# Attention and a Toeplitz convolution on one core: two further Toeplitz tile buffers, second buffers for the conv's result and taps, a longer planned slack, and a tail in halves

## The chip, the core and the metric

The kernel runs on one core of a Trainium2 chip. The metric is the device time of one execution in microseconds; several executions are timed, and the median is given. A profile is taken of one execution by the hardware profiler. The engines are PE (matmuls; PEld is its weight load), ACT, DVE, POOL, and SP, which here only issues DMAs.

## The reference

Two branches over 2048 tokens with 448 channels are mixed by a gate of each token (bf16 inputs and output):

```
g = sigmoid((x * gate_w).sum(-1, keepdims=True))
a = A(x)      # 16 heads of 28, one shared key and value head: softmax(q k^T / sqrt(28)) v, then @ wo
b = B(x)      # per channel d: K[d,l] = Re sum_n C[d,n] exp(dt*A[d,n]*l) dt*B[d,n], causal conv of x with K, plus x * Dskip
out = g * a + (1 - g) * b
```

In B, n runs over 256 complex modes, and the convolution has the full length of 2048.

## The kernel before, in words

**Attention.** Index i = 0 to 15 stands for a chunk of 512 queries (i // 4) and a group of four heads (i % 4). Its 64 tiles (16 key blocks x 4 heads) give 1024 score tiles in all, taken in sets of three and two in turn. For each set PE computes scores (L1138) into PSUM banks 0 to 5, ACT takes the exponential of the whole set into a ring of 15 slots (L1162, 410 instructions), and PE multiplies by the values with a column of ones for the denominators (L1171) into bank psB. After 16 key blocks `norm(i)` (L1045) copies psB to `acc` (L1051, on ACT) and, for i < 15, sends the denominators through DRAM to come back broadcast: DMA to denT, reciprocal (L1058), DMA to R, DMA to rdenB, multiply to onT (L1062). The DMAs are POOL's. `outp` (L1027) multiplies four onT by Wo, and `fold` (L1039) adds gate times the result to O on DVE (L1042).

**Convolution.** Channels are taken 32 at a time, c = 0 to 13. `masters` and `tables` build powers of the modes on DVE (L848 to L927), `kgen` (L930) sums them to taps on PE (L948), DVE and ACT evict these to `kstg` (L958, L961), and POOL writes them to KP in DRAM. From there `tload` (L974) reads Toeplitz tiles: tile gi = 0 to 111 holds four channels, 128 partitions by 4288 bf16 values, with shifted overlapping reads of KP; SP issues these loads into T, which has NTR = 5 slots, gi % 5. `conv` (L982) takes four tiles: 4 x 8 groups of four matmuls (L995) into one of two PSUM banks that kgen, the query projection `qproj` (L798), outp and conv share; DVE multiplies by 1 - g into `cst` (L1005), PE transposes cst (L1016), and DVE adds to O (L1024). There is one cst, so the first matmul of conv(c) waits for the transposes of conv(c - 1). Channel block 13 is built in two halves (`HALVES`); its tables run in 64 columns at a time.

**Tail.** For i = 15 there is no DMA in norm: DVE copies psB (L1052), PE sums the denominators with selecting columns (L1070), DVE takes reciprocals (L1074) and spreads them to 512 columns (L1076), PE transposes them back (L1081), DVE multiplies (L1085). `tail` (L1088) multiplies the last chunk's onT by Wo for four token tiles: three heads groups early, the fourth after L1085 (both L1103); four folds follow (L1042), then the output DMAs. All four depend on the key ("O", 3), and so on all four folds.

**What sets the order.** Nothing is ordered by hand. `Prog.op` and `Prog.dma` record operations with a cost in ns, keys read and written, and a priority; `schedule` (L147) plays them through and takes again and again the operation that can start first (ties by priority). So each engine's instruction order comes from these costs. An operation of PE with priority 1.2 or more, or DVE with 2 or more, is taken to be ready later than its inputs by a slack, 700 ns on PE and 300 on DVE, unless `slk` names another:

```
if x.pr >= (1.2 if x.eng == "pe" else 2) or x.slk:
    t += self.SLACK.get(x.eng, 0.0) if x.slk is None else x.slk
```

A DMA's cost (L139, L226) is a time on the shared engines plus 2200 ns plus its `extra`; for a T load that is 2584 + 2200 + 2500. `emit` then writes the orders out with semaphore waits. Each engine executes its list in order, so an instruction that waits holds all behind it. `fill` (L616) puts matmuls that add zero (L632) into gaps of PE's plan, to keep its clock up.

Of the kernel before, what the change touches and what calls it, by code (L numbers as in the profile page):

```python
# [11 lines left out]
P = 128  # L12
# [20 lines left out]
NTR = 5  # L33
RING = 15
# [3 lines left out]
NCST = 1  # L38
# [313 lines left out]
def on(i):  # L352
    return i % NON


class Kernel:
# [34 lines left out]
    def alloc(self):  # L391
# [25 lines left out]
        self.T = sb("T", NTR * TW, BF)  # L417
        self.tab = sb("tab", 2 * LO + 32 * EW, BF)
        self.tmp = sb("tmp", 2 * 8 * EW, BF)
# [11 lines left out]
        self.cst = sb("cst", NCST * 512, BF)  # L431
        self.skt = sb("skt", D // 4, BF)
        self.small = sb("small", 16, F32)
        self.gt = sb("gt", 2 * 16, F32)
# [5 lines left out]
    def consts(self):  # L440
# [6 lines left out]
        dm(V(self.kstg, 0, 256), 0.0, 170, [("kst", 0), ("kst", 1)])  # L447
# [33 lines left out]
    def loads(self):  # L481
# [41 lines left out]
        for k in range(2, 6):  # L523
# [7 lines left out]
               (448, 128), "pad", rd=[("kst", 0), ("kst", 1)], wr=["pad"], pr=3)  # L531
# [15 lines left out]
    def prep_x(self):  # L547
# [3 lines left out]
        for q in range(4):  # L551
            for hp in range(2):
# [11 lines left out]
                dst = xT.v(0, DT, 2 * hp * S + 512 * q, [[S, 2], [4, 128], [1, 4]])  # L564
# [9 lines left out]
            def mk(e, q=q, t=t, o=o):  # L574
                for T in range(NT):
                    r = e.matmul(t.v(0, P, o, [[1, 512]]), self.Wk.v(0, DT, T * P, [[1, P]]),
                                 xT.v(0, DT, T * S + 512 * q, [[1, 512]]),
                                 start=(T == 0), stop=(T == 3), tile_position=(0, 0))
                return r
# [9 lines left out]
            def mv(e, q=q):  # L589
                for kt in range(4 * q, 4 * q + 4):  # L590
                    for T in range(NT):
                        r = e.matmul(self.psB.v(0, P, 32 * kt, [[1, 29]]), xT.v(0, DT, T * S + 128 * kt, [[1, 128]]),
# [18 lines left out]
        pg.op("dve", lambda e: e.tensor_scalar(og, g, -1.0, 1.0, ALU.mult, ALU.add), 80, rd=["gt"], wr=["og"], pr=1)  # L611

# [185 lines left out]
    def qproj(self, i):  # L798
# [8 lines left out]
        for T in range(NT):  # L807
            pg.op("pe", lambda e, T=T: e.matmul(
                px(), self.Wq.v(0, DT, T * 512 + g * 128, [[1, 128]]),
                self.xT.v(0, DT, T * S + 512 * qc, [[1, 512]]), start=(T == 0), stop=(T == 3),  # L810
# [119 lines left out]
    def kgen(self, c, sub=None):  # L930
# [9 lines left out]
        k1, k2 = ([(k, h) for h in ((0, 1) if whole else (sub,))] for k in ("kst", "kst2"))  # L940
        for jj in range(8):
# [13 lines left out]
            for comp in range(2):  # L955
                pg.op("pe", lambda e, mm=mm, comp=comp: mm(e, comp), 226 if whole else 113, mode="c", st=2.08 if whole else 1.04,
                      rd=keys, wr=[X] + k1 + k2, pr=1.7, lock=G if jj == 0 and comp == 0 else None)
        pg.op("dve", lambda e: e.tensor_tensor(self.kstg.v(p0, np, 63, [[64, 8]]), G.v(p0, np, 63, [[64, 8]]),  # L958
                                               self.skt.v(p0, np, 8 * c, [[1, 8]]), ALU.add),
              el(8), rd=[X, "skt"], wr=k1, pr=2)  # L960
        pg.op("act", lambda e: e.activation(self.kstg.v(p0, np, 0, [[64, 8], [1, 63]]), G.v(p0, np, 0, [[64, 8], [1, 63]]), AF.Copy),  # L961
              490, rd=[X] + k1, wr=k2, pr=-1, unlock=G)
        ko = self.kstg
        rs = ko.rs
        lst = [(dram(self.KP, (32 * c + 8 * gs[0]) * KW + 1024, [[8 * KW, len(gs)], [KW, 8], [1, 64]]),
                bass.AP(tensor=ko.h, offset=(p0 + 16) * rs, ap=[[32 * rs, len(gs)], [64, 8], [1, 64]]))]
        for g in gs:
            for h in range(2):
                lst.append((dram(self.KP, h * KH + (32 * c + 8 * g) * KW, [[64, 16], [KW, 8], [1, 64]]),
                            ko.v(32 * g + 16 * h, 16, 0, [[64, 8], [1, 64]])))  # L970
        pg.dma(lst, (264 * len(gs), 128), f"kw{sub or 0}", rd=k1 + k2, wr=[("KP", 2 * c + h) for h in ((0, 1) if whole else (sub,))],
               pr=0, eng="pool", extra=2000)

    def tload(self, gi):  # L974
        pg = self.pg
        s = gi % NTR
        x = ["tpdone", "rawdone"] if gi < NTR else []
        pg.dma([(self.T.v(0, P, s * TW, [[1, TW]]),
                 dram(self.KP, 4 * gi * KW, [[1, 64], [KH, 2], [1, TW]]))],
               (128, 2 * TW), f"T{s}", rd=[("KP", gi // 4), "pad"] + x, wr=[("T", s)], pr=1, extra=2500)  # L980

    def conv(self, c):  # L982
        pg = self.pg
        X = ("cx", c)
        co, ck = 512 * (c % NCST), ("cst", c % NCST)
# [3 lines left out]
        for k in range(4):  # L989
            gi = 4 * c + k  # L990
            s = gi % NTR
            for n in range(8):
                def mm(e, k=k, n=n, s=s, gi=gi):
                    for j in range(4):
                        r = e.matmul(ps.v(32 * j, 32 - 2 * n, 128 * k, [[1, 128]]),  # L995
                                     self.U.v(0, P, 2 * n * D + 4 * gi + j, [[D, 32 - 2 * n]]),
                                     self.T.v(0, P, s * TW + j * KW + 896 - 128 * n, [[1, 128]]),
# [5 lines left out]
                      wr=[X] + ([ck] if first else []), pr=1.8,  # L1003
                      lock=ps if first else None)
        pg.op("dve", lambda e: e.tensor_tensor(self.cst.v(0, P, co, [[128, 4], [64, 2], [1, 64]]),  # L1005
# [5 lines left out]
        def yt(e, k):  # L1011
            for par in range(2):
                for mu in (0, 1):
# [3 lines left out]
                                 self.cst.v(0, P, co + 128 * k + 64 * (1 - mu), [[1, 64]]),  # L1017
# [27 lines left out]
    def norm(self, i):  # L1045
# [5 lines left out]
        (pg.op("act", lambda e: e.activation(av, self.psB.v(0, P, 0, [[1, 512]]), AF.Copy), 490, rd=[("b", 6)], wr=[ak], pr=-1) if i < 15 else  # L1051
         pg.op("dve", lambda e: e.tensor_copy(av, self.psB.v(0, P, 0, [[1, 512]])), el(512), rd=[("b", 6)], wr=[ak], pr=0))  # L1052
# [204 lines left out]
```

## Time and profile before

| | |
|---|---|
| runs | 542.43, 543.3, 543.5, 547.04, 548.25 us; median 543.5 |
| profiled execution | 542.43 us, span 540.7 us |
| mean granted PE clock | 0.961 |
| first and last exponential (L1162) | 26.03 us to 528.08 us |
| T loads | 112 of 1072 KB, issued from 94.4 to 511.6 us; issue to landing 5.8 / 10.5 / 20.0 us (least, median, most) |
| conv matmuls (L995) | 2048 into psX, 1536 into psS, 0.24 us each |
| last transposes of the conv (L1016) | end at 527.8 us |

The profile is read so. Busy time of an engine is summed over its instructions; the span is that of the profiled execution. A line like "L1162 ACT ACTIVATE expT<-psS" names a line of the code, the engine, the operation and the tiles it writes and reads; "x410" counts instructions, then come busy us and mean ns of one, then the idle time just before them and who ended most of it. "issue" means that the engine waited for nothing that the profile shows. The granted clock is a share of PE's full clock, the DMA share the mean busy share of the core's 16 DMA engines.

### The profile page before, as it was taken

Reading aid. Unit: us, or ns where it says so; the run is one execution under the profiler, and the core shown is the slowest. Engines: PE = TensorE matmul, PEld = TensorE weight load, DVE = VectorE, ACT = ScalarE, POOL = GpSimd, SP = SyncE. Lnnn points to the kernel's source line nnn. Section 1 sums busy time; section 2 is a strip of 40 time slices with the busy share of each in tenths; the row PEclk is TensorE's granted clock in tenths of the full one; section 3 lists DMA queues with packets and bytes.
Section 4 is the critical chain, followed back from the end, with each engine's and each line's share of the span. In section 5 each row is a group of like instructions: output and inputs, shape, how many; then the busy total and the mean of one; then the engine's idle time right before and its main releaser. Section 6 shows DMA issues by size and latency. Waiting matters only on the chain.

```text
span 540.7 us, 20290 instructions
## 1 busy us (share of the span) xinstructions
PE 485.0 (90%) x9244; PEld 247.4 (46%) x9259; DVE 449.8 (83%) x885; ACT 497.3 (92%) x457; POOL 102.1 (19%) x192
## 2 busy tenths in 40 slices
PE   7689898989999899999899999899988999997984
PEld 4432243344445444554455554454544455553442
DVE  8979999989989799999999999999999997211113
ACT  3799999988989799999999999999999999799890
POOL 2000004003022304004040404022041330401000
PEclk9999999997979799999999989999999999899898
DMA  8931100996945978897877979979978879599954
GB/s 233 283 121 52 31 23 13 342 308 220 365 160 193 347 281 309 325 359 279 337 282 264 313 282 347 359 295 344 359 270 336 280 243 396 159 369 351 392 209 136
DMA packets 38382, 142.88 MB, mean 264 GB/s; under 512 B 10580, under 2 KB 21372, under 8 KB 23960
## 3 DMA queue, kind: packets, MB, share of 16 engines
q1 hardware_dynamic: 27656, 135.29, 69.1%
q0 software_dynamic: 9104, 6.13, 4.5%
q8 instruction: 72, 1.18, 0.9%
q10 hardware_dynamic: 1536, 0.17, 0.3%
q14 instruction: 14, 0.11, 0.1%
HBM read 135.38 MB, written 5.74 MB: 261 GB/s over the span
## 4 chain that ended last, share of the span: by engine, by line
ACT 43%; PE 25%; DVE 17%; DMA 13%; issue 1%; ACTq 0%; another core or an unknown queue 0%
ACT expT L1162 41%; PE psS L1138 7%; DMA T<-KP_scratch 7%; PE psS L948 6%; PE psB L1171 4%; DMA rdenB<-R_scratch 3%; DVE tab L903 2%; PE psS L995 2%; DMA sz<-in_A_wv_dram 2%; PE psX L995 1%; PE psX L948 1%; DVE tab L910 1%; DVE tab L909 1%; DVE tab L922 1%; DVE tmp L905 1%
## 5 line engine op out<-in xcount | busy, mean ns | idle before, releaser
L1162 ACT ACTIVATE expT<-psS 128x1536 bf16<-128x1536 f32 (+1 forms) x410 | 470.8, 1330 | 15.1 <-PE psS L1138 13.9
L1138 PE MATMUL psS<-qT,kT 32*128 32x512 bf16 x1024 | 164.6, 396 | 26.6 <-ACT expT L1162 19.6
L1171 PE MATMUL psB<-expT,vaug 128*32 128x512 bf16 x1024 | 105.2, 401 | 0.7 <-ACT expT L1162 0.3
L1138 PEld LDWEIGHTS psS<-qT,kT 32*128 32x128 bf16 x1024 | 39.4, 91 | 116.3 <-ACT expT L1162 91.6
L137 POOL DMA_DIRECT2D KP_scratch<-kstg x127 | 68.3, 546 | 87.8 <-ACT kstg L961 86.0
L1144 PE MATMUL psB<-ident,zero 32*128 32x512 bf16 x190 | 75.3, 396 | 0.0
L903 DVE TENSOR_TENSOR tab<-tab,mbf 128x256 bf16<-128x256 bf16 (+5 forms) x75 | 69.4, 926 | 1.1
L995 PE MATMUL psX<-T,U 128*26 128x128 bf16 (+7 forms) x2048 | 59.1, 244 | 4.7 <-DMA T<-KP_scratch 3.7
L995 PEld LDWEIGHTS psX<-T,U 128*26 128x26 bf16 (+7 forms) x2048 | 51.1, 162 | 16.9 <-issue 9.0
L632 PE MATMUL psB<-ident,zero 128*32 128x512 bf16 (+3 forms) x808 | 55.6, 337 | 0.2 <-issue 0.2
L1171 PEld LDWEIGHTS psB<-expT,vaug 128*32 128x32 bf16 x1024 | 26.3, 93 | 60.4 <-issue 58.6
L948 PE MATMUL psS<-tab 128*32 128x64 bf16 x1024 | 46.0, 294 | 3.2 <-issue 2.9
L995 PE MATMUL psS<-T,U 128*32 128x128 bf16 (+7 forms) x1536 | 43.4, 241 | 4.2 <-issue 2.7
L995 PEld LDWEIGHTS psS<-T,U 128*32 128x32 bf16 (+7 forms) x1536 | 38.2, 162 | 12.5 <-issue 8.3
L948 PEld LDWEIGHTS psS<-tab 128*32 128x32 bf16 x1024 | 34.2, 138 | 13.7 <-issue 10.4
L905 DVE TENSOR_TENSOR tmp<-tab,mbf 128x256 bf16<-128x256 bf16 (+4 forms) x62 | 39.6, 638 | 0.0
L137 POOL DMA_DIRECT2D denT<-acc x15 | 10.7, 714 | 138.8 <-ACT acc L1051 138.8
L922 DVE TENSOR_TENSOR tab<-tab,tmp 128x2048 bf16<-128x2048 bf16 x28 | 33.5, 1222 | 0.4
L137 POOL DMA_DIRECT2D R_scratch<-denT x15 | 8.7, 578 | 130.0 <-DVE denT L1058 87.9
L948 PE MATMUL psX<-tab 128*32 128x64 bf16 x768 | 31.3, 292 | 0.9 <-issue 0.7
L1005 DVE TENSOR_TENSOR cst<-psX,omq 128x512 bf16<-128x512 f32 x16 | 11.0, 686 | 23.8 <-PE psX L995 23.7
L905 DVE TENSOR_TENSOR tab<-tab,mbf 128x4096 bf16<-128x4096 bf16 x13 | 29.7, 2284 | 0.0
(145 smaller groups left out, 547.6 us busy)
## 6 DMA issues: line engine op xcount, KB each, us to landing
T<-KP_scratch SPq DMA_DIRECT2D x112, 1072.0 KB, 10.6
rdenB<-R_scratch POOLq DMA_DIRECT2D x15, 256.0 KB, 11.9
U<-in_A_x_dram SPq DMA_DIRECT2D x3, 896.0 KB, 15.8
tab<-in_A_x_dram SPq DMA_DIRECT2D x4, 448.0 KB, 7.2
KP_scratch<-kstg POOLq DMA_DIRECT2D x112, 16.0 KB, 5.1
SZ_scratch<-tab SPq DMA_DIRECT2D x1, 1344.0 KB, 5.8
out_dram<-O SPq DMA_DIRECT2D x3, 448.0 KB, 3.8
sz<-SZ_scratch SPq DMA_DIRECT2D x3, 384.0 KB, 3.3
```

Of the source, the lines that this page charges most:

```text
L137: return [e.dma_start(o, i, **kw) for o, i in pairs]
L632: r = e.matmul(t.v(32 * j, 32, bo, [[1, 128 * m]]), self.zero.v(0, P, 0, [[1, 32]]), self.ident.v(0, P, 0, [[0, m], [1, P]]), start=not ac ...
L903: vo(lambda e, dst=dst, src=src, mr=mr: e.tensor_tensor(dst, src, mr, ALU.mult), 2 * n, done + mk(lv), kr + ki)
L905: vo(lambda e, src=src, mi=mi, w=w, n=n, tb=tb, to=to: e.tensor_tensor(tb.v(0, P, to, [[n, 2], [cw, w], [1, cw]]), src, mi, ALU.mult), 2 * ...
L922: vo(lambda e, h=h: e.tensor_tensor(tab.v(0, P, FM + 32 * h, [[64, 2], [EW, 32], [1, 32]]), tab.v(0, P, lo + 31 * EW + 64 * h, [[BLK, 2], ...
L948: r = e.matmul(G.v(32 * g, 32, 64 * jj, [[1, 64]]), tab.v(0, P, lo + comp * BLK + 32 + o, [[EW, 32]]), tab.v(0, P, fo, [[mo - fo, 2], [EW, ...
L995: r = e.matmul(ps.v(32 * j, 32 - 2 * n, 128 * k, [[1, 128]]), self.U.v(0, P, 2 * n * D + 4 * gi + j, [[D, 32 - 2 * n]]), self.T.v(0, P, s ...
L1005: pg.op("dve", lambda e: e.tensor_tensor(self.cst.v(0, P, co, [[128, 4], [64, 2], [1, 64]]), ps.v(0, P, 63, [[128, 4], [64, 2], [-1, 64]]) ...
L1138: r = e.matmul(self.psS.v(0, P, 512 * (bo + k), [[1, 512]]), kT.v(32 * h, 32, 128 * kt, [[1, 128]]), qT.v(32 * h, 32, 512 * (i % 2), [[1, ...
L1144: r = e.matmul(self.psB.v(0, P, 0, [[1, 512]]), self.zero.v(32 * h, 32, 0, [[1, P]]), self.ident.v(32 * h, 32, 0, [[0, 4], [1, P]]), start ...
L1162: pg.op("act", lambda e: e.activation(expT.v(0, P, 512 * es, [[1, n]]), self.psS.v(0, P, 512 * bo, [[1, n]]), AF.Exp, scale=SQ), 50 + n / ...
L1171: r = e.matmul(self.psB.v(32 * h, 32, 0, [[1, 512]]), vaug.v(0, P, 32 * kt, [[1, 32]]), expT.v(0, P, 512 * (t % RING), [[1, 512]]), start= ...
```

## The change

- **Toeplitz slots.** `self.tslots` holds the five slots of T, a sixth in xT (columns 1856 to 6143, from tile 70 on) and a seventh at the start of tab (from tile 96 on). `slot` gives a tile the slot used longest ago among those open to it. The first load into either new slot waits for the last readers of the old contents: the query projections of the first three quarters of xT, and the readers of the even tables. To this end xT is laid out by quarters of tokens (2048 q + 512 T in place of 2048 T + 512 q), and all its readers are changed to match.
- **Second buffers.** Odd c in `conv` uses xT columns 0 to 511 as cst, odd c in `kgen` uses columns 512 to 1023 as kstg. Both wait, at c = 1, for the readers of xT's first quarter.
- **Slack.** The first group (n = 0) of matmuls on each Toeplitz tile gets slk = 2500.
- **Gate into the normalisation for i = 12 to 15.** Two small DMAs on SP write the last chunk's gates to DRAM and read them back as gtT; for i = 12 to 14 denT is multiplied by it. The tail then needs no gate.
- **norm(14)** copies psB on DVE instead of ACT.
- **Tail in halves.** For i = 15 copy, denominator sums, reciprocal, spreading (now times the gate) and multiplication are done on 256 columns at a time. In `tail`, PE adds O to each token tile's product by an identity matmul; ACT and DVE take turns in copying the result to O; each output DMA depends on its own tile alone.

The diff, cut to its core (left out are the new address forms of xT's other readers, the constants and some key names):

```diff
+        self.tslots = [(self.T, s * TW, ["tpdone", "rawdone"]) for s in range(NTR)]
+        self.tslots.append((self.xT, NT * S - TW - 2048, [("xT", hp, q) for hp in range(2) for q in range(3)]))
+        self.tmap, self.tlast = {}, [s - 9 for s in range(NTR)] + [-20, -20]
...
+        self.tslots.append((self.tab, 0, [("lo", 0, k) for k in range(13)]))
...
-                dst = xT.v(0, DT, 2 * hp * S + 512 * q, [[S, 2], [4, 128], [1, 4]])
+                dst = xT.v(0, DT, 2048 * q + 1024 * hp, [[512, 2], [4, 128], [1, 4]])
...
+        pg.dma([(dram(self.R, 15 * 2048, [[1, P], [128, 4]]), self.gt.v(0, P, 12, [[1, 4]]))], (512, 4), "gw", rd=["gt"], wr=["GT"], pr=4, slow=True)
+        pg.dma([(self.gtT.v(0, P, 0, [[1, 16]]), dram(self.R, 15 * 2048, [[0, 4], [16, 32], [1, 16]]))], (128, 64), "gr", rd=["GT"], wr=["gtT"], pr=4)
...
+        k1, k2 = ([(k, h, c % 2) for h in ((0, 1) if whole else (sub,))] for k in ("kst", "kst2"))
+        ko, ks = ((self.kstg, 0), (self.xT, 512))[c % 2]
+        if c == 1:
+            k1 += [("xT", hp, 0) for hp in range(2)]
...
+    def slot(self, gi):
+        if gi not in self.tmap:
+            av = [s for s in range(len(self.tslots)) if gi >= (0, GX, GT)[max(0, s - NTR + 1)]]
+            self.tmap[gi] = min(av, key=lambda s: self.tlast[s])
+            self.tlast[self.tmap[gi]] = gi
+        return self.tmap[gi]
...
-        s = gi % NTR
-        x = ["tpdone", "rawdone"] if gi < NTR else []
-        pg.dma([(self.T.v(0, P, s * TW, [[1, TW]]),
+        s = self.slot(gi)
+        t, o, x = self.tslots[s]
+        x, y = ([], x) if s >= NTR else (x, []) if gi < NTR else ([], [])
+        pg.dma([(t.v(0, P, o, [[1, TW]]),
...
+        cb, co = ((self.cst, 0), (self.xT, 0))[c % 2]
+        ck, cx = ("cst", c % 2), [("xT", hp, 0) for hp in range(2)] if c == 1 else []
...
+                      wr=[X] + ([ck] + cx if first else []), pr=1.8,
+                      slk=2500 if n == 0 else None,
...
+        if i < 14:
+            pg.op("act", lambda e: e.activation(av, self.psB.v(0, P, 0, [[1, 512]]), AF.Copy), 490, rd=[("b", 6)], wr=[ak, kb], pr=-1)
+        elif i == 14:
+            pg.op("dve", lambda e: e.tensor_copy(av, self.psB.v(0, P, 0, [[1, 512]])), el(512), rd=[("b", 6)], wr=[ak, kb], pr=0)
...
+            if i > 11:
+                pg.op("dve", lambda e: e.tensor_tensor(dv, dv, self.gtT.v(0, P, 0, [[1, 16]]), ALU.mult), 80, rd=["dn", "gtT"], wr=["dn"], pr=1)
...
-        pg.op("dve", lambda e: e.tensor_copy(self.rdenB.v(0, P, 0, [[32, 16], [1, 32]]), self.denT.v(0, P, 0, [[1, 16], [0, 32]])),
-              el(512), rd=["dn"], wr=["rd"], pr=0)
...
+        for h in range(2):
+            av = self.acc.v(0, P, ao + 256 * h, [[1, 256]])
+            src = self.psB.v(0, P, 256 * h, [[1, 256]])
+            pg.op("dve", lambda e, a=av, b=src: e.tensor_copy(a, b), el(256), rd=[("b", 6)], wr=[kb if h else ak], pr=0)
+        for h in range(2):
+            b0, b1 = ((0, 1), (6, 0))[h]
...
+            pg.op("dve", lambda e, h=h: e.tensor_tensor(
+                self.rdenB.v(0, P, 256 * h, [[128, 2], [32, 4], [1, 32]]), self.denT.v(0, P, 8 * h, [[4, 2], [1, 4], [0, 32]]),
+                self.gt.v(0, P, 12 + 2 * h, [[1, 2], [0, 4], [0, 32]]), ALU.mult), el(256), rd=["dn", "gt"], wr=[("rd", 1) if h else "rd"], pr=0)
...
+            pg.op("pe", lambda e, px=px, ov=ov: e.matmul(px(), self.ident.v(0, P, 0, [[1, P]]), ov, start=False, stop=False,
+                                                         tile_position=(0, 0), skip_group_check=True), 200,
+                  rd=["id", ("O", 3)], wr=[X] + key, pr=0.8)
...
-            self.fold(3, tt, px, 0, D, [X], unlock=G)
+            if tt % 2:
+                pg.op("dve", lambda e, px=px, ov=ov: e.tensor_copy(ov, px()), el(D), rd=[X], wr=[("Ox", tt)], pr=0, unlock=G)
+            else:
+                pg.op("act", lambda e, px=px, ov=ov: e.activation(ov, px(), AF.Copy), 430, rd=[X], wr=[("Ox", tt)], pr=0, unlock=G)
...
-                   (128, 896), f"out{tl}", rd=[("O", 3)], pr=1)
+                   (128, 896), f"out{tl}", rd=[("Ox", tt)], pr=1)
```

## The prediction

> **What bounds the kernel now.** I read the busy shares first, then ACT's waits, then the stretches around each of those waits, then the last 13 us. The busy shares:
>
> ```profile
> PE 485.0 (90%) x9244; PEld 247.4 (46%) x9259; DVE 449.8 (83%) x885; ACT 497.3 (92%) x457; POOL 102.1 (19%) x192
> L1162 ACT ACTIVATE expT<-psS 128x1536 bf16<-128x1536 f32 (+1 forms) x410 | 470.8, 1330 | 15.1 <-PE psS L1138 13.9
> ```
>
> ACT carries the stream of exponentials (L1162). By its timeline that stream starts at 26.03 us and ends at 528.08. By the table of stretches ACT is busy for 482.6 of these 502.05 us, so 19.4 us of idling is all that the middle can give. Ahead of it lie 26 us that the change leaves alone, behind it 12.6 us of tail. Who makes ACT idle (waits of ACT, total, times, longest):
>
> ```profile
> ACT expT L1162 <- PE psS L1138: 13.9, 18, 2.2
> ACT kstg L961 <- DVE kstg L958: 2.7, 2, 2.1
> ```
>
> It is the score matmuls (L1138), that is, PE having been late. The stretches tell why (columns: length, PE, PEld, DVE, ACT and POOL busy, granted clock, DMA share, GB/s):
>
> ```profile
> 118.00:121.00 3.00, 1.57 (x11) 0.46 (x11) 3.00 (x10) 0.93 (x3) 0.00 (x0) 0.75 0.85 283
> 121.00:126.00 5.00, 4.53 (x37) 1.47 (x40) 4.18 (x9) 4.09 (x4) 4.92 (x9) 0.50 0.63 174
> ...
> 461.00:465.00 4.00, 4.00 (x70) 3.25 (x70) 0.00 (x0) 1.85 (x3) 1.76 (x4) 0.91 0.29 80
> ...
> 497.00:501.00 4.00, 0.64 (x15) 0.34 (x19) 0.00 (x0) 2.91 (x4) 0.69 (x1) 1.00 1.00 306
> 501.00:505.00 4.00, 4.00 (x60) 1.34 (x55) 1.38 (x2) 2.71 (x3) 0.00 (x0) 0.60 1.02 355
> ```
>
> Three kinds of loss. (a) Five times (119, 150, 178, 317 and 413 us) PE stands still for 0.6 to 1.6 us with nothing visible to wait for ("issue"); after the three longer pauses its granted clock is 0.50 to 0.66 for 6 to 10 us and ACT loses more. Together, by the gaps in ACT's timeline, 4.0 + 2.0 + 3.1 + 1.3 + 0.7 = 11.1 us. (b) Around the half-width kernel generation of c = 13 (452 to 470 us) 4.1 us: 28 of its matmuls take 1.72 us, where 32 full-width ones took 1.13. (c) At 497.6 us PE waits for a Toeplitz tile:
>
> ```profile
> 500.76 0.56 PE L995 MATMUL psX<-T,U 128*32 128x128 bf16 x16 [3.15 <-DMA T<-KP_scratch]
> 501.25 0.39 PE L1138 MATMUL psS<-qT,kT 32*128 32x512 bf16 x2
> 501.56 0.41 PE L1171 MATMUL psB<-expT,vaug 128*32 128x512 bf16 x4
> 501.68 1.02 ACT L1162 ACTIVATE expT<-psS 128x1024 bf16<-128x1024 f32 x1 [1.77 <-PE psS L1138]
> ```
>
> The scores queued behind that conv are late, and ACT idles 1.77 and then 0.61 us: 2.4 us. The other 1.8 us are scattered. Last, the tail:
>
> ```profile
> 528.58 0.69 DVE L1052 COPY acc<-psB 128x512 f32<-128x512 f32 x1 [1.83 <-PE psB L1171]
> 529.32 1.06 PE L1070 MATMUL psS<-msq,acc 128*128 128x4 f32 x8
> 530.24 1.86 PE L1103 MATMUL psS<-Wo,onT 128*128 128x448 bf16 x9
> 531.93 1.05 PE L1081 MATMUL psS<-msq,rdenB 128*128 128x128 f32 x8
> 533.03 0.69 DVE L1085 TENSOR_TENSOR onT<-acc,psS 128x512 bf16<-128x512 f32 x1 [1.89 <-PE psS L1081]
> 534.17 2.84 DVE L1042 SCALAR_TENSOR_TENSOR O<-psS,gt,O 128x448 bf16<-128x448 f32 x4 [0.46 <-PE psS L1103]
> 537.04 1.80 SPq L137 DMA_DIRECT2D out_dram<-O  x4
> ```
>
> A serial chain: no output DMA is issued before the fourth fold ends, at 537.0 us.
>
> **What the Trainium skill says.** "TensorE: Matmul & The Clock Gate", What's actually happening: PE falls to half clock after an idle window of about 3.4 us and needs about as long a busy one to come back. The trace agrees on the level (0.50 at 121 to 126 us), but here pauses of only 1.5 us bring it on. "Runtime: NRT & Kernel Launch", Instruction fetch mechanics: instructions arrive in 16 KiB blocks over a DMA queue of the sequencer's own, mostly hidden. The page's queue table has 72 packets and 1.18 MB for instructions, 16 KiB each, which agrees; that the pauses (a) are such fetches delayed by loaded DMA engines (share 0.85 to 1.0 there) fits, but nothing here shows it. "VectorE: DVE Perf Modes", The perf-mode tier table: an fp32 copy from SBUF runs at 2x, a tensor_tensor only at 1x. The trace agrees: L1076 copies 512 in 0.43 us, L851 takes 0.42 for 256.
>
> **The change part by part.**
>
> *Toeplitz buffers, second cst and kstg, slack.* The same 112 loads of 1.07 MB, the same 3584 conv matmuls, the same 13 kernel evictions and 28 L1005: no work goes away. What moves is when. SP issues six T loads from 440.7 us, two at 466.6 and fifteen from 474.1, the last at 511.6; the DMA share is only 0.29 at 461 to 465 us and then 1.0 at 374 to 383 GB/s from 480 to 520. So the late tiles are bandwidth-bound because slots were full while DMA idled. Two more slots from tile 96 let two loads go before the rush: 2 x 1.1 MB / 0.38 = about 6 us less backlog. The plan also starts each tile 2500 ns after its planned landing instead of 700, 1.8 us more, and a conv no longer waits for the previous one's L1005 and transposes. PE's wait at 497.6 us was 3.15 us: 1.8 plus part of 6 covers it. ACT's 2.4 us could come back wholly, or not at all if the plan only packs convs closer to the landings; I take 2.0. What is late next is ACT itself, which runs without a gap from 503.3 to 528.1 us already. The pauses (a) and the half-width loss (b) aren't touched. The slack costs nothing while PE has other work: the last transposes now end at 527.8 us, just before the last exponential, and two early tiles bring them forward by about 6 us against the 1.8 us that slack adds. Without that cover, up to 1.8 us.
>
> *kgen(1) and conv(1)* gain a dependency on xT's first quarter, and so on each other: kgen(1)'s matmuls now follow conv(1)'s first. At worst that puts kgen(1), and with it DVE's table chain, some us back; T loads end some 6 us earlier, which hides it. Nil; if uncovered, a few us of DVE chain that ended at 467 us, 60 us before ACT.
>
> *Two gate DMAs* on SP's queue (512 descriptors of 4 bytes, and 128 of 64). They wait for DVE's gate reciprocal, and behind them on SP are seeds, pads and later the T loads, of which the first is issued at 94.4 us. Before that SP's and the DMA engines' load is light (DMA share 0.18 at 57 to 100 us). Nil; uncovered, the nearest row (denT, 64-byte pieces) lands in 6.2 us. The three extra multiplies of 16 columns (L1058's reciprocal of the same size is 0.25 us) lie in a chain of about 28 us. Nil. xT's new layout changes no element count.
>
> *Norm of i = 14 by DVE.* ACT loses one L1051, whose next instruction started 0.47 us after it; DVE, idle for 8 to 10 us around there, takes it in 0.69 (L1052's row). Gain 0.5 us, between 0 and 0.6.
>
> *Tail.* Per half: copy 0.42 (256 columns, as L1024), four sum matmuls 0.53 (half of L1070), reciprocal 0.25, broadcast now a tensor_tensor of 256, 0.42 (the whole copy had 0.43, so the broadcast gets no shorter per half), four back matmuls 0.53, multiply 0.42. Staggered from the last L1171's end at about 528.5: half copies end 529.0 and 529.4; sums 529.75 and 530.3 (behind the three L1103 that sit there now); broadcasts 530.5 and 531.2; PE slips in a group of three L1103 (0.62) before the back matmuls, which end 531.5 and 532.05; multiplies 532.0 and 532.55. PE then owes one more group, the rest of four new identity matmuls (0.21 each by L1103's 1.86/9) and four last-head matmuls: about 2.0 us, to 534.1. The last copy (0.68 on DVE; ACT takes two of the four, 0.60 each by L961) ends 534.8. Its DMA is issued alone: the four now take 1.80 us to issue, so it starts at once instead of 1.35 us late, and the end comes about 2.3 us later (0.45 to issue, 1.85 to land): 537.1 against 540.7, 3.6 us. If PE has to do all groups after 532, 2.7; if all wait ahead of the last exponential, 4.4. I take 3.5.
>
> Sum: 3.5 + 2.0 + 0.5 = 6.0. The span goes from 540.7 to 534.7; the profiled execution's time, 1.7 above its span, from 542.4 to 536.4. The median shown, 543.5, is 1.1 above that execution and two of its five runs are over 547; I put the forecast at 536.5.
>
> **Rivals.** *Only the tail pays:* the stall (c) reappears at another tile, since the plan books 2.6 us of DMA per tile and the rush really takes 1.07 MB / 0.38 = 2.9, so landings fall behind it by 0.3 us per tile, 2.4 after eight. Then 3.5 + 0.5, at 538.5 to 539.5. For it: slack is gone after some eight tiles of rush; against: fewer tiles wait in the rush. *More comes back:* the new order on PE puts block borders and half-width bursts elsewhere; of (a) and (b), 15 us together, a third is saved: 531.5. For it: late in the run only 317 and 413 us have a pause; against: no edit aims at them. *Slower: more PE pauses.* One pause with its slow clock costs 11.1 / 5 = 2.2 us on ACT; with up to seven T loads in flight the DMA engines are full more of the time, from 340 us on. From three further pauses on, 6.6 us, the gain is eaten: 543.5 and above; six would be 549 and more. Against: between 300 and 460 us the share is 0.84 to 0.99 already and only two pauses are there.
>
> **How the numbers follow.** This measurement can tell about 1%, 5.4 us, from no change: faster is below 538.1, slower above 548.9. Chances: the forecast 0.48 (own range 533.5 to 539.5, four parts in five of it below 538.1), more comes back 0.20, only the tail 0.20, more pauses 0.12, about half of it above 548.9. Faster 0.38 + 0.20 + 0.02 = 0.60, same 0.10 + 0.18 + 0.05 = 0.33, slower 0.07. The range 531.0 to 543.5 leaves about one in ten out at either end.
>
> **What would show it.** Right: last exponential to the end of the span about 9 us, not 12.6; output DMAs issued one by one, not together; no PE wait for T above 1 us after 470 us; the last L1016 well before the last L1162; ACT idle between first and last L1162 about 17 us. Wrong: more or longer "issue" pauses with a clock near 0.5 after 340 us; L1062 of i = 14 (at 526.1 us now, 2.4 us before L1103 needs it) landing late behind T loads, or the fold's identity matmul waiting for the last conv, either of which holds the tail.

## The result and the profile after

| | before | after |
|---|---|---|
| median of the runs | 544.38 us (44 runs) | 538.81 us (23 runs) |
| profiled execution, its span | 542.43, 540.7 us | 536.94, 535.2 us |
| first to last exponential ("the middle") | 502.0 us | 499.1 us |
| ACT busy, idle in the middle | 482.6, 19.4 us | 481.5, 17.5 us |
| last exponential to the end ("the tail") | 12.6 us | 9.8 us |
| PE waiting for a T tile | 4.0 us | 0.0 us |
| T loads: last issued at | 511.6 us | 495.5 us |

The ratio of the times, after to before, is 0.9912, with a 95% interval of 0.9888 to 0.9936: 0.9% faster, just inside the 1% that the prediction took as its border. The span fell by 5.5 us: 2.9 in the tail, 3.0 in the middle, 0.4 given back because the first exponential starts later. The lines of the code have moved; the exponential is now L1205, the scores L1181, the values L1214, the conv L1015, its transposes L1037, the Wo matmuls L1140. The same two rows of the page as before, of the kernel after:

```profile
PE 482.1 (90%) x9171; PEld 247.3 (46%) x9186; DVE 449.5 (84%) x891; ACT 497.3 (93%) x458; POOL 102.1 (19%) x192
L1205 ACT ACTIVATE expT<-psS 128x1536 bf16<-128x1536 f32 (+1 forms) x410 | 470.6, 1338 | 16.5 <-PE psS L1181 12.0
```

ACT's work is what it was, and before the exponentials it waits 16.5 us where it waited 15.1. The waits of ACT (total, times, longest):

```profile
ACT expT L1205 <- PE psS L1181: 12.0, 18, 1.5
...
ACT expT L1205 <- PE psB L1187: 3.9, 5, 1.2
...
ACT xT L972 <- DVE xT L969: 1.0, 2, 0.7
```

The score matmuls make it wait 12.0 us instead of 13.9, but the zero-adding matmuls put behind them (L1187) 3.9 instead of 0.6. What ACT saves lies elsewhere: by its timeline it stands 2.7 us before its evictions of taps in the middle where now it is 1.0, and 2.9 us before its copies of psB where now it is 1.6. What made PE late is in PE's waits:

```profile
PE psX L1015 <- issue: 2.8, 2, 1.7
...
PE psB L1214 <- issue: 2.1, 2, 1.8
...
PE psS L1037 <- issue: 1.7, 1, 1.7
```

No row for T is left; before, PE waited 3.7 and 0.3 us for T. "issue" remains, and is not smaller. The stretches of the kernel after (columns as in the prediction) show how the late loads moved:

```profile
461.00:465.00 4.00, 3.75 (x73) 2.37 (x66) 0.57 (x2) 3.75 (x4) 0.00 (x0) 1.00 1.02 390
470.00:525.46 55.46, 49.91 (x995) 24.61 (x992) 12.10 (x23) 55.45 (x50) 5.70 (x10) 1.00 0.79 287
510.00:520.00 10.00, 8.91 (x187) 4.12 (x179) 1.11 (x2) 10.00 (x10) 0.70 (x1) 1.00 0.10 32
```

At 461 to 465 us the DMA share is 1.02 where it was 0.29, and at 510 to 520 it has fallen to 0.10. From 470 us to its last exponential ACT is busy for 55.45 of 55.46 us. The last transposes end at 519 us, 6 us before the last exponential; before, they ended 0.3 us before it. Last, the tail, by the timeline of the kernel after (the last exponential ends at 525.45):

```profile
525.95 0.76 DVE L1095 COPY acc<-psB 128x256 f32<-128x256 f32 x2 [6.34 <-PE psB L1214]
...
526.62 0.68 DVE L1088 TENSOR_TENSOR onT<-acc,rdenB 128x512 bf16<-128x512 f32 x1
...
527.36 0.74 PE L1140 MATMUL psS<-Wo,onT 128*128 128x448 bf16 x3
...
529.39 0.42 DVE L1120 TENSOR_TENSOR onT<-acc,psS 128x256 bf16<-128x256 f32 x1 [0.28 <-PE psS L1116]
...
531.27 0.73 PE L1140 MATMUL psX<-Wo,onT 128*128 128x448 bf16 x3
...
532.42 0.62 DVE L1151 CAST O<-psX 128x448 bf16<-128x448 f32 x1 [1.27 <-PE psX L1140]
```

The halves follow each other as foreseen, but all four groups of Wo matmuls come after the last exponential: L1088, the multiplication for i = 14 that they need, stands behind the copies L1095 on DVE. It did not wait for its data: the broadcast that it reads had landed at 516.7 us.

One of the kernels below, late_only, needs a word: 13 of its 20 executions lie over 1.5% above its fastest (536.2 us), its ratio rests on the other seven, and its two traces are of the longer kind.

### The profile page after: what moved, and what is told of

Read it like the earlier page. It is cut to its first block, busy times and chain, and to the rows that moved or that the text cites. A ratio compares the mean times of both kernels' runs of the same rounds, so it can differ in the third digit from the quotient of the medians.

```text
span 535.2 us, 20165 instructions
## 1 busy us (share of the span) xinstructions
PE 482.1 (90%) x9171; PEld 247.3 (46%) x9186; DVE 449.5 (84%) x891; ACT 497.3 (93%) x458; POOL 102.1 (19%) x192
## 4 chain that ended last, share of the span: by engine, by line
ACT 56%; PE 21%; DVE 13%; DMA 8%; issue 2%; ACTq 0%; another core or an unknown queue 0%
ACT expT L1205 54%; PE psS L1181 6%; PE psB L1214 4%; PE psX L959 3%; DMA rdenB<-R_scratch 3%; DMA denT<-acc 2%; DMA sz<-in_A_wv_dram 2%; PE psX L1015 2%; DVE tab L911 2%; PE psS L1015 1%; PE psS L959 1%; ACT acc L1074 1%; DMA R_scratch<-denT 1%; DVE msq L856 1%; DVE tab L913 1%
## 5 line engine op out<-in xcount | busy, mean ns | idle before, releaser
L1205 ACT ACTIVATE expT<-psS 128x1536 bf16<-128x1536 f32 (+1 forms) x410 | 470.6, 1338 | 16.5 <-PE psS L1181 12.0
L1181 PE MATMUL psS<-qT,kT 32*128 32x512 bf16 x1024 | 164.8, 396 | 33.1 <-ACT expT L1205 23.2
L1214 PE MATMUL psB<-expT,vaug 128*32 128x512 bf16 x1024 | 105.5, 401 | 2.6 <-issue 2.1
L1181 PEld LDWEIGHTS psS<-qT,kT 32*128 32x128 bf16 x1024 | 39.4, 91 | 120.3 <-ACT expT L1205 98.3
L1187 PE MATMUL psB<-ident,zero 32*128 32x512 bf16 x190 | 75.0, 395 | 0.0
L1015 PE MATMUL psX<-T,U 128*18 128x128 bf16 (+7 forms) x1920 | 53.9, 240 | 3.5 <-issue 2.8
L1214 PEld LDWEIGHTS psB<-expT,vaug 128*32 128x32 bf16 x1024 | 26.4, 93 | 63.7 <-issue 61.7
L1015 PEld LDWEIGHTS psX<-T,U 128*18 128x18 bf16 (+7 forms) x1920 | 47.1, 162 | 13.7 <-issue 10.0
L640 PE MATMUL psB<-ident,zero 128*32 128x512 bf16 (+3 forms) x728 | 48.7, 337 | 0.0
L138 POOL DMA_DIRECT2D KP_scratch<-xT x64 | 34.5, 546 | 42.5 <-ACT xT L972 42.5
L138 POOL DMA_DIRECT2D KP_scratch<-kstg x63 | 34.2, 551 | 34.5 <-ACT kstg L972 32.8
L1015 PE MATMUL psS<-T,U 128*32 128x128 bf16 (+7 forms) x1344 | 39.5, 241 | 0.6 <-issue 0.3
L959 PE MATMUL psX<-tab 128*32 128x64 bf16 x960 | 39.7, 293 | 0.0
L1015 PEld LDWEIGHTS psS<-T,U 128*32 128x32 bf16 (+7 forms) x1344 | 33.6, 161 | 9.4 <-issue 7.4
L959 PE MATMUL psS<-tab 128*32 128x64 bf16 x832 | 35.3, 293 | 0.3 <-DVE tab L918 0.3
L959 PEld LDWEIGHTS psX<-tab 128*32 128x32 bf16 x960 | 30.3, 138 | 6.5 <-issue 3.9
L959 PEld LDWEIGHTS psS<-tab 128*32 128x32 bf16 x832 | 26.5, 138 | 7.4 <-issue 5.4
## 6 DMA issues: line engine op xcount, KB each, us to landing
rdenB<-R_scratch POOLq DMA_DIRECT2D x15, 256.0 KB, 11.7
```

Of the source, the lines that this page charges most:

```text
L138: return [e.dma_start(o, i, **kw) for o, i in pairs]
L640: r = e.matmul(t.v(32 * j, 32, bo, [[1, 128 * m]]), self.zero.v(0, P, 0, [[1, 32]]), self.ident.v(0, P, 0, [[0, m], [1, P]]), start=not ac ...
L959: r = e.matmul(G.v(32 * g, 32, 64 * jj, [[1, 64]]), tab.v(0, P, lo + comp * BLK + 32 + o, [[EW, 32]]), tab.v(0, P, fo, [[mo - fo, 2], [EW, ...
L1181: r = e.matmul(self.psS.v(0, P, 512 * (bo + k), [[1, 512]]), kT.v(32 * h, 32, 128 * kt, [[1, 128]]), qT.v(32 * h, 32, 512 * (i % 2), [[1, ...
L1187: r = e.matmul(self.psB.v(0, P, 0, [[1, 512]]), self.zero.v(32 * h, 32, 0, [[1, P]]), self.ident.v(32 * h, 32, 0, [[0, 4], [1, P]]), start ...
L1205: pg.op("act", lambda e: e.activation(expT.v(0, P, 512 * es, [[1, n]]), self.psS.v(0, P, 512 * bo, [[1, n]]), AF.Exp, scale=SQ), 50 + n / ...
```

## The experiments

Questions: is the tail's gain separate from the rest; did the late package (slots, second buffers, slack) bring the 3.0 us of the middle by ending the stall at T; is each of its parts worth something alone; what are the "issue" pauses; why did the tail bring 2.9 and not 3.5?

| kernel | ratio to before, 95% interval | span | middle | ACT idle in it | tail | PE waits for T |
|---|---|---|---|---|---|---|
| after | 0.9912 (0.9888 to 0.9936) | 535.2 | 499.1 | 17.5 | 9.8 | 0.0 |
| tail_only | 0.9937 (0.9909 to 0.9966) | 539.7 | 503.7 | 21.5 | 9.8 | 3.3 |
| late_only | 0.9953 (0.9913 to 0.9994), seven runs | 548.6 | 509.7 | 27.1 | 12.6 | 0.0 |
| late_again | one run, 550.2 us | 548.5 | 509.8 | 27.4 | 12.6 | 0.0 |
| no_slots | 1.0121 (1.0029 to 1.0213) | 545.7 | 508.0 | 26.6 | 11.4 | 1.1 |
| no_slack | 1.0080 (1.0048 to 1.0111) | 549.0 | 512.7 | 29.6 | 9.8 | 8.9 |
| no_buf2 | 1.0121 (1.0028 to 1.0213) | 552.3 | 508.7 | 26.1 | 17.2 | 0.0 |
| light_before | 0.9644 (0.9574 to 0.9713) | 524.2 | 485.5 | 5.6 | 12.6 | 0.0 |
| light_T | 0.9612 (0.9549 to 0.9674) | 519.2 | 483.0 | 3.9 | 9.8 | 0.0 |
| light_no_slots | 0.9843 (0.9805 to 0.9881) | 536.0 | 498.5 | 18.6 | 11.2 | 0.0 |
| split_T | 0.9984 (0.9956 to 1.0012) | 540.3 | 500.3 | 18.9 | 13.9 | 5.0 |
| early14 | 0.9810 (0.9714 to 0.9906) | 529.5 | 494.5 | 13.2 | 8.6 | 1.0 |
| early14_5 | 0.9836 (0.9775 to 0.9896) | 534.2 | 498.9 | 17.0 | 9.1 | 0.0 |

Middle, idle time, tail and waits are read from one execution each. Single executions of the kernel before lie between 538.9 and 553.8 us, so a difference of a few us between two middles says little by itself.

**tail_only** keeps norm and tail of the kernel after and takes slots, second buffers and slack away.

```diff
-GX = 70
-GT = 96
+GX = 1000
+GT = 1000
-        ko, ks = ((self.kstg, 0), (self.xT, 512))[c % 2]
+        ko, ks = self.kstg, 0
-        cb, co = ((self.cst, 0), (self.xT, 0))[c % 2]
+        cb, co = self.cst, 0
-                      slk=2500 if n == 0 else None,
+                      slk=None,
```

> The kernel before with only the new tail: halves, gate in the normalisation, norm(14) on DVE; five Toeplitz slots, one conv result and one taps buffer, 700 ns of slack (xT keeps its new layout). My theory: the gain is a sum of two separate parts, so here the tail (last exponential to the end) is 9.5 to 10 us as after the whole change, not 12.6, and the stretch from first to last exponential is as before: about 502 us, with a PE wait for a Toeplitz tile of 1 us or more after 470 us. Time about 3 us below before, ratio 0.994. Rival (the tail only pays because the convs end early): the tail is 11 us or more, since the identity matmuls wait for the last conv, and the ratio is about 1.

Its tail is 9.8 us, as in the kernel after, so the tail's gain of 2.9 us needs nothing of the late package. PE waits for T again, 3.3 us in two waits, but not where I had expected it, after 470 us:

```profile
184.72 0.63 PE L1013 MATMUL psS<-T,U 128*32 128x128 bf16 x16 [2.31 <-DMA T<-KP_scratch]
...
353.54 0.63 PE L1013 MATMUL psS<-T,U 128*32 128x128 bf16 x20 [1.00 <-DMA T<-KP_scratch]
```

So this plan has no stall in the last rush even with five slots. Its median is 541.91 us (20 runs). Its interval overlaps that of the kernel after; that the late package adds anything to the tail's gain (0.25%, 1.4 us, by the two ratios) is not shown.

**late_only** and **late_again** (the same kernel) keep the late package and take norm and tail of before, without the gate DMAs.

```diff
-        if i < 14:
-            pg.op("act", lambda e: e.activation(av, self.psB.v(0, P, 0, [[1, 512]]), AF.Copy), 490, rd=[("b", 6)], wr=[ak, kb], pr=-1)
...
+        pg.op("act", lambda e: e.activation(av, self.psB.v(0, P, 0, [[1, 512]]), AF.Copy), 490, rd=[("b", 6)], wr=[ak, kb], pr=-1)
```

> The whole change but for the tail: seven Toeplitz slots, second buffers, 2500 ns of slack; the tail, the fold and norm(14) as before. My theory: tail 12 to 12.6 us; no PE wait for a Toeplitz tile over 0.5 us after 470 us; ACT without a gap over 0.3 us from 470 us to the last exponential; time about 2 us below before, ratio 0.996. Rival (the middle's difference is only where the issue pauses fall): ACT's idling between first and last exponential is 19 us or more again, ratio 1.00.

> The same kernel as late_only (seven Toeplitz slots, second buffers, 2500 ns of slack; old tail), for a profile of a further execution. My theory: tail 12 to 12.6 us; no PE wait for a Toeplitz tile over 0.5 us after 470 us; ACT idles 16 to 19 us between first and last exponential, and where its issue pauses fall partly differs from the first execution though every instruction is the same. Rival (pauses belong to places in the program): the same pauses at the same instructions.

No wait for T, as expected, but no gain that can be shown: the median of all its runs is 546.7 us against 545.1 for the kernel before beside it. The traced executions idle 27 us on ACT, where 16 to 19 were expected, and ACT has gaps of up to 1.8 us after 470 us, where none over 0.3 was. Both executions took 550 us, over the median, so the 10 us by which they idle more than the kernel after, whose late package is the same, are no measure of the kernel. PE's pauses have a part in them: in the waits of PE, `PE psX L1013 <- issue` is 9.5 us in late_only and 9.1 in late_again. Where the two traces pause is the point of late_again. I count PE's matmuls and weight loads from the start to each pause and divide by 256. First the kernel after, then late_only (stretches from 0 to the pause; the counts are the x of PE and PEld):

```profile
0.00:304.01 304.01, 272.36 (x4938) 133.20 (x4947) 287.46 (x567) 284.69 (x263) 58.38 (x116) 0.96 0.67 234
0.00:364.63 364.63, 327.29 (x6086) 162.80 (x6097) 344.77 (x690) 342.47 (x316) 72.23 (x140) 0.96 0.72 250
0.00:423.14 423.14, 381.28 (x7234) 192.14 (x7247) 401.15 (x783) 399.27 (x368) 85.22 (x164) 0.96 0.73 260
```

```profile
0.00:366.86 366.86, 325.18 (x6086) 161.72 (x6097) 347.26 (x693) 343.41 (x317) 71.81 (x140) 0.97 0.72 251
```

9885, 12183 and 14481 instructions make 38.61, 47.59 and 56.57 blocks of 256; a fourth pause comes at 60.55. late_only and late_again have their four longest pauses at the same four places (some matmul records are missing from the traces; by the weight loads alone the counts are equal), for 1.47, 3.04, 2.15, 2.32 and for 1.57, 2.63, 1.92, 2.22 us. This is what the rival of late_again foresaw. Of their shorter pauses of 0.5 us or more, two are at common places too, and each trace has one of its own. The kernel before paused at 11.69, 15.68, 19.66, 37.61, 40.60 and 55.56. All these have nearly the same remainder, 0.55 to 0.69: the pauses stand at borders of 256 PE instructions, at places fixed by the program.

**light_before** and **light_T** cut every T load but the first into each slot to 64 of its 4288 columns, in the kernel before and in the kernel after; the conv so runs on stale data, with the same instructions. (light_T: the same with `first` for the first use of a slot.)

```diff
-        pg.dma([(self.T.v(0, P, s * TW, [[1, TW]]),
-                 dram(self.KP, 4 * gi * KW, [[1, 64], [KH, 2], [1, TW]]))],
+        n = TW if gi < NTR else 64
+        pg.dma([(self.T.v(0, P, s * TW, [[1, n]]),
+                 dram(self.KP, 4 * gi * KW, [[1, 64], [KH, 2], [1, n]]))],
```

> The changed kernel, in which a Toeplitz load moves its full 4288 columns only at the first use of each slot and 64 columns afterwards, so it leaves out most of the convolution's data; planner's costs and so every engine's order are unchanged. If the issue pauses of PE are instruction blocks delayed by loaded DMA engines (my theory), they nearly vanish here: PE's issue waits above 0.5 us fall from 6 to 0 or 1, the clock stays at 1.0, ACT idles 6 to 9 us between first and last exponential instead of about 16, and the time is 530 us or less. Rival (the pauses belong to PE's instruction stream, whatever the DMA load): as many pauses, ACT idling 14 us or more, time within 2 us of the changed kernel's.

> The kernel before, in which a Toeplitz load moves its full 4288 columns only at the first use of each slot and 64 columns afterwards, so it leaves out most of the convolution's data; every engine's order is that of before. Without loaded DMA engines the two plans are compared bare. My theory: PE's issue pauses and its waits for T vanish, about 13 us; the half-width loss around c = 13 stays; first to last exponential takes 488 to 490 us, 2 us or less more than in the changed kernel treated the same way (its 483), the tail stays 12.5 us, and the time is 526 to 529 us. Rival (the new order on PE is better in itself, not by T): first to last exponential differs by 4 us or more between the two.

The stretch of the middle, of light_before and then of light_T:

```profile
26.11:511.56 485.45, 451.48 (x9022) 231.28 (x9035) 420.31 (x836) 479.90 (x441) 97.95 (x172) 0.99 0.15 38
```

```profile
26.38:509.41 483.03, 446.64 (x8945) 230.57 (x8958) 420.44 (x840) 479.18 (x440) 98.17 (x172) 0.99 0.17 46
```

With the DMA share at 0.15 and 0.17, the granted clock is 0.99, no pause over 0.3 us is left, and ACT idles 5.55 and 3.85 us (6 to 9 were expected of light_T). So in the traced executions the loads cost ACT 19.43 - 5.55 = 13.9 us before and 17.54 - 3.85 = 13.7 after: the stall at T is gone, and what the loads cost in all is the same. One execution each carries no more than that: by the ratios the loads cost 3.6% before (1 - 0.9644) and 3.0% after (0.9912 - 0.9612), each uncertain by 0.7 points, so a saving of some us is not excluded. The 3.0 us of the middle are mostly there without loads in these traces: 485.45 - 483.03 = 2.4 us, between the 2 of my theory and the 4 of its rival; 0.7 of it is ACT's own work and 1.7 idle, of which the gaps around the half-width kernel generation give most (3.2 us before, 1.7 after). But the traced execution of light_before, 525.9 us, is the longest of its four. The medians, 524.9 and 521.1 us, differ by 3.8 us; 2.9 of that is the tail, which leaves about 0.9 for the middle. Pauses need both: a border in the program, and loaded DMA engines.

**no_slots**, **no_slack** and **no_buf2** each take one part out of the kernel after, as in tail_only's diff. **light_no_slots** is light_T without the two slots.

> The changed kernel with the five Toeplitz slots of before; second buffers, 2500 ns of slack and the new tail stay. My theory (the two extra slots let loads run ahead before the last rush): the last T load is again issued after 505 us, PE waits for a Toeplitz tile after 470 us for 1 to 2 us in all, ACT loses 1 to 2.4 us there, and the time is 1 to 2 us above the changed kernel's. Rival (the slack alone covers the late landings): no wait for a Toeplitz tile over 0.5 us, time as the changed kernel's within 1 us.

> The changed kernel with the slack of 700 ns on Toeplitz tiles as before; seven slots, second buffers and the new tail stay. My theory (slots and slack each cover part): PE waits for Toeplitz tiles several times, 2 to 5 us in all over the run, because second buffers let the plan pack convs right behind the planned landings; the time is 1 to 3 us above the changed kernel's. Rival (the slots alone suffice): waits under 1 us in all, same time.

> The changed kernel with one conv result buffer and one taps buffer; seven slots, 2500 ns of slack and the new tail stay. My theory (a conv's start after the previous transposes was covered by other PE work): time within 1 us of the changed kernel's, no wait for a Toeplitz tile over 0.5 us; the last conv transposes end some us later, before the last exponential. Rival (without the second buffer the slack pushes the convs past the end): the last L1016 ends after the last exponential and the tail grows by 1 us or more.

> no_slots with Toeplitz loads of 64 columns after each slot's first, which leaves out most of the convolution's data. It asks whether the 11 us that no_slots costs over the changed kernel lie in its plan or in late landings. Theory A (late landings: with five slots held 1.8 us longer, T loads crowd and everything behind PE slips): bare of DMA load it takes 521 us or less, within 2 us of light_T's 519.2 span. Theory B (the plan itself is worse: it puts an ACT eviction ahead of the taps that it waits for, and a norm's multiply too late): the ACT gap of 8 us before the copy of psB is there again and the time is 526 us or more.

Each is 9 to 12 us slower than the kernel after by the medians (549.9, 548.1 and 550.5 us; four runs each of no_slots and no_buf2), and slower than the kernel before. None was expected over 3 us slower. The waits for T came as foreseen in no_slots and were larger in no_slack; of no_buf2 the rival, a longer tail, came true. Without the slack, PE stands at T; waits of PE, then ACT in the timeline, no_slack:

```profile
PE psX L1015 <- DMA T<-KP_scratch: 6.2, 4, 2.3
...
PE psS L1015 <- DMA T<-KP_scratch: 2.7, 2, 1.9
```

```profile
196.04 2.44 ACT L1205 ACTIVATE expT<-psS 128x1536 bf16<-128x1536 f32 x2 [5.07 <-PE psS L1181]
```

The largest loss is at 192 to 196 us, nowhere near the end. The plan books 7.3 us for a T load; here they land after 11.5 us (median), and a slack of 0.7 us covers less of the difference than 2.5. Without second buffers, waits of PE and a late line of the timeline, no_buf2:

```profile
PE psX L957 <- DMA KP_scratch<-kstg: 5.2, 4, 3.4
```

```profile
543.93 0.45 PE L1035 MATMUL psS<-ident,cst 128*64 128x64 bf16 x16 [0.81 <-DVE cst L1024]
```

The kernel generation waits for kstg to be written out, and the last conv's transposes end 9 us after the last exponential (535.2 us): the tail takes 17.2 us. Without the slots, T is not what is late (1.1 us). Waits of ACT, no_slots and then light_no_slots:

```profile
ACT acc L1074 <- DVE onT L1088: 8.4, 1, 8.4
ACT xT L972 <- DVE xT L969: 5.9, 2, 4.7
```

```profile
ACT acc L1076 <- DVE onT L1090: 7.0, 1, 7.0
ACT xT L972 <- DVE xT L969: 4.8, 2, 4.5
```

Both gaps remain with small loads, and the middle is still 498.5 - 483.0 = 15.4 us longer than light_T's. So they are in the plan: with five slots and the slack it puts 102 kernel-generation matmuls on PE in one burst of 3.2 us at 402 us, and the copy of psB behind DVE's L1088. That the plan does this is shown; why was not traced. A rival stays open for all three: the kernel after may be a well-drawn plan, and any change of its costs might lose as much. split_T, next, takes no part out and lies about 4 us above it by the ratios.

**split_T** issues each T load as four DMAs of 1072 columns.

```diff
-        pg.dma([(t.v(0, P, o, [[1, TW]]),
-                 dram(self.KP, 4 * gi * KW, [[1, 64], [KH, 2], [1, TW]]))],
+        n = TW // 4
+        pg.dma([(t.v(0, P, o + n * j, [[1, n]]),
+                 dram(self.KP, 4 * gi * KW + n * j, [[1, 64], [KH, 2], [1, n]])) for j in range(4)],
```

> The changed kernel with each Toeplitz load issued as four DMAs of 1072 columns in place of one of 4288; the same bytes, descriptors a quarter as long. If instruction blocks are delayed because they wait behind long descriptors, the pauses shrink: issue waits of PE above 0.5 us fall from 8 us in all to 4 or less and the time by 2 to 5 us. Rival (what counts is how full the DMA engines are, not the length of a descriptor): pauses as before, the loads a little slower, time within 2 us or above the changed kernel's.

Two long pauses of 3.0 us together instead of five of 7.0, as expected, but 5.0 us of waiting for T, and a late conv makes the tail 13.9 us. The time does not fall: the ratio, 0.9984 (0.9956 to 1.0012), lies above that of the kernel after; since the plan changed with the issues, whether smaller pieces shorten the pauses stays open.

**early14**, and **early14_5** (the same, in five rounds), shorten the planned slack in norm(14) and let the first and last token tile have the free banks.

```diff
-            pg.op("dve", lambda e: e.reciprocal(dv, dv), 160, rd=["dn"], wr=["dn"], pr=1, slk=SLK[0])
+            pg.op("dve", lambda e: e.reciprocal(dv, dv), 160, rd=["dn"], wr=["dn"], pr=1, slk=1000 if i == 14 else SLK[0])
...
-                  el(512), rd=[ak, kb, "rd", "onw"], wr=[("on", on(i))], pr=2, slk=SLK[1])
+                  el(512), rd=[ak, kb, "rd", "onw"], wr=[("on", on(i))], pr=2, slk=500 if i == 14 else SLK[1])
...
-            if tt < 3:
+            if tt in (0, 3):
```

> The changed kernel with the planned slack of norm(14)'s reciprocal cut from 4000 to 1000 ns and of its last multiply from 4000 to 500 ns, and with the four tail tiles in PSUM banks 4, pool, pool and 2 instead of 2, 3, 4 and pool. In the changed kernel PE sits idle for much of 520 to 525 us and then does all four groups of three heads after the last exponential, because the multiply of i = 14 is planned behind the tail's copies (526.6 us). My theory: PE sets the pace of the tail, so with the groups done ahead the tail falls from 9.7 to 7.5 to 8 us, ratio to before about 0.987. Rival (the chain copy, sums, reciprocal, spread, back, multiply on DVE and PE sets the pace): the tail stays above 9 us.

> The same kernel as early14 (norm(14) planned earlier, tail tiles in other banks), in more rounds, because its first interval came from few executions. Tail theory: last exponential to the end 8.6 us as before in early14, not 9.7; ratio to before 0.980 to 0.988. If the first result was a lucky draw of PE's pauses: ratio 0.989 or above, no better than the changed kernel's 0.9912 by more than 1.1 us.

The tail by the timeline of early14:

```profile
514.93 0.68 DVE L1088 TENSOR_TENSOR onT<-acc,rdenB 128x512 bf16<-128x512 f32 x1
...
521.79 0.76 DVE L1095 COPY acc<-psB 128x256 f32<-128x256 f32 x2 [6.17 <-PE psB L1214]
...
525.09 0.42 DVE L1120 TENSOR_TENSOR onT<-acc,psS 128x256 bf16<-128x256 f32 x1 [0.28 <-PE psS L1116]
...
526.16 0.62 DVE L1151 CAST O<-psS 128x448 bf16<-128x448 f32 x1
```

L1088 now runs 6 us before the last exponential ends, and groups of three Wo matmuls from 516.6 us. From the start of the copies L1095 to the end of the last copy to O it takes 526.78 - 521.79 = 5.0 us instead of 533.04 - 525.95 = 7.1. The tail is 8.6 and 9.1 us in the two traces: less than 9.8, not the 7.5 to 8 that I had expected, since the chain from copy to second multiplication (3.7 us, 3.9 in the kernel after) stays. The two edits, slack and banks, were not tried apart. At 0.9836 (0.9775 to 0.9896; median 536.51) it is the fastest kernel here that moves all its data; its interval overlaps that of the kernel after, so that it beats the latter is likely, not settled. The tail gives about 1 us of the 4 between the two ratios; the rest, if it is there, lies in the middle.

## Why the prediction was right, and where not

- **Size of the whole.** Foreseen -6.0 us of span; measured -5.5, and by the ratio -4.8 us (3.5 to 6.1) of 544.4. The median came out 2.3 us above 536.5. About 2.0 of this is the base: I took the sum from one execution of 542.4 and did not add what the median lies above it (1.1 by the runs shown, 1.95 by the 44 now there). The mistake made "faster by over 1%" look likelier than it was. That the span came so near is in part luck: the 2.0 us of the stall were met by savings elsewhere, as below, and what the tail lacked by ACT's shorter work.
- **Tail, -3.5: right mechanism, mis-sized term; -2.9.** The chain was right: its second multiplication ends 3.9 us after the last L1214, 4.05 foreseen. The output DMAs are issued one after another, and the end comes 2.2 us after the last copy (2.3). The failing term is "PE slips in a group of three L1103": L1088 of i = 14 came too late, and PE did all groups afterwards, the case priced at 2.7. The prediction named a late landing as what could do this; in fact the broadcast landed 9.9 us before L1088 ran, the DMA share was 0.10, and the order on DVE was planned so. early14, where L1088 runs first, has 0.7 to 1.1 us less tail.
- **Stall at T, -2.0: the stall went, the reason for the sum did not hold.** PE waits 0.0 us for T, ACT runs without a gap from 470 us, and the loads are earlier, all as written. ACT's idle time fell by 1.9 us, but that this meets the 2.0 is luck: the light pair of traces puts the cost of the loads at 13.9 us before and 13.7 after. ACT got late elsewhere: the pauses sum to 7.0 us (5.6 before). And at 119 us the broadcast of i = 1's denominators lands 14.3 us after its issue (issued 105.1); DVE, its table chain and PE wait, the clock falls to 0.66, and ACT loses 4.0 us at 118 to 138 us. The slots were meant to end the stall; in the finished plan it is above all the slack that keeps PE from standing at T (8.9 us without it, 1.1 without the slots, none without the second buffers). As far as the middle is shorter at all (3.0 us in the traces, 2.4 in the light pair, less by its medians), this rests on the plan: smaller gaps at the half-width generation, which the prediction had called untouched, and ACT's shorter work.
- **norm(14) on DVE, -0.5: right.** ACT has one copy fewer, and 1.1 us less to do in the middle (0.7 in the light pair). What was missed comes later in the same norm: its L1088 held back the Wo groups of the tail. Whether the copy's move to DVE has a share in that was not tried.
- **Slack "costs nothing", second buffers as a detail: wrong as prices of parts.** In the finished plan, taking out the slack costs about 9 us, the second buffers 12, the slots 11 (differences of medians). The prediction priced a sum of parts with one plan in mind; each part changes the whole plan. Alone, each looked like 0 to 2 us.
- **Pauses "not touched": wrong in place, nearly right in sum.** They moved from mostly before 180 us to 227, 304, 365, 423 and 449 us. The rival "more PE pauses" did not come true in the kernel after (five of 7.0 us against six of 5.6, where the prediction had counted five, without the one at 298 us) but it did in the two traces of late_only: four of 9.0 and of 8.3 us between 300 and 460 us. It was no far-off case: the late package is the same.
- **The rivals.** "Only the tail pays" named T waits at another tile; there are none. "More comes back" needed 5 us from pauses and half-width bursts; about 1.5 came from the latter.

"Runtime: NRT & Kernel Launch", Instruction fetch mechanics, has the block of 16 KiB as 256 instructions. That PE's pauses keep to borders of 256 agrees with it, and with 72 fetches for some 18,360 PE instructions. Its "mostly hidden" does not hold under load: up to 3.0 us of PE at one border here. The prediction held that nothing shows the fetch itself, but the traces hold it: each fetch is one packet of 16 KiB on the queue "instruction" (q8). The kernel after, in us from the start:

| PE stops | packet of q8, start to end | PE goes on | after the packet's end |
|---|---|---|---|
| 226.63 | 224.60 to 225.80 | 227.25 | 1.45 |
| 302.34 | 301.75 to 302.70 | 304.06 | 1.37 |
| 363.00 | 361.82 to 363.20 | 364.68 | 1.48 |
| 421.36 | 420.72 to 421.79 | 423.19 | 1.40 |
| 447.63 | 446.18 to 447.18 | 448.75 | 1.57 |

In the eleven traces with full loads there are 56 pauses of 0.5 us or more, and after each of them PE goes on 1.3 to 1.6 us after such a packet has ended: the pause is the wait for the fetch. The packet itself takes about 1.0 us (median) with full loads and with small ones. What differs is its start: 3.2 us after PE passed the border before it in the kernel before, 0.6 in light_before (medians; an estimate, with the borders set where the pauses stand).

## What to carry to other kernels

Where a planner sets every engine's order, take each part out of the finished kernel as well as adding it alone: three parts that seemed worth 0 to 2 us each cost 9 to 12 when missing here. A stall that disappears is no gain until the idle time of the bounding engine says so; a copy of the kernel with small transfers gives what the transfers cost in all. In a tail, look first at what could have run before the last instruction of the bounding engine, and at which planned order kept it back.

## What the hardware showed that was not expected

- PE's pauses stand at some of the borders of 256 of its instructions, and only under load: 0.5 to 3.0 us each with T loads of 1072 KB, none over 0.3 us with 16 KB. Each ends 1.3 to 1.6 us after a packet of instructions has landed.
- Landing times under load and light (medians of the kernel after and light_T): rdenB, 256 KB, 11.7 against 5.0 us; denT 6.5 against 2.2 us; R 5.6 against 1.9 us. A DMA on the path takes two to three times as long beside full queues.
